# A new order of the right-hand columns, other first and last blocks, and one projection group of a slot added to x from PSUM by VectorE: window attention with a convolution on one core

## The chip, the cores and the metric

One core of a Trainium2 chip runs the kernel. The metric is the device time of one execution in microseconds, the median of three runs. Engines are named as in the profile: PE is TensorE (PEld its weight loads), DVE VectorE, ACT ScalarE, POOL GpSimd, SP the sync engine, which here only issues DMAs.

## The reference

The input x is an image of 511 x 511 positions with 192 channels in bf16. The result is

```
pe  = depthwise 3x3 convolution of x (zero border), weights dw_pe
x0  = x + pe
h   = layernorm(x0) over the channels, no scale or bias
windows of 7x7 positions: 73 x 73 windows of 49 tokens
qkv = h @ w_qkv          # 4 heads of 48
out = softmax(q k^T / sqrt(48)) v @ w_o, per window and head
return x0 + out
```

## The kernel before, in words

**Blocks.** The 73 x 73 windows are handled in blocks of up to 128 windows, one window in each partition. `_blocks` (L42) lists the lines of windows of which a block consists: (first row, first column, row step, column step, number of windows, first partition). There are 42 blocks. Blocks 0 to 35 hold two half rows of 64 windows each (columns 0 to 63). Block 36 holds row 72's half and a part of column 64, blocks 37 to 40 two pieces of columns of 64 windows each (rows 1 to 64), and block 41 the nine corners that are left: nine lines of 9 windows, 81 in all.

**What a block needs.** `load_xp` (L203) fills XP: for each window the 9 x 9 patch of x that the convolution reads, 81 partitions. It issues nine loads for each line, one for each patch column, in runs of 384 bytes, and clears patches at the image's border by a DMA of zeros (L200). There is one XP buffer. `load_x` (L248) loads x itself into X[b % 3], 14 strips in a block of two lines, and one piece for each line in a block of more than two. `store` (L300) writes the result from X in four chunks of rows, one DMA for each line and chunk. All of these wait in order in SP's queue, and each DMA uses one of eight semaphores and waits for the earlier DMA of its semaphore.

**The convolution** (`conv_mm`, L311) is a matmul for each channel, 192 in a block. Ten channels fill a `psc` buffer in PSUM, of which there are two; VectorE adds it to X (L324). Then come layernorm statistics on VectorE (L329), the inverse deviation on GpSimd (L338, L339), the norm (L344, mostly GpSimd), transposes into HO on TensorE (L354) and copies out of PSUM (L364).

**The slots.** The main loop (from L563) runs over 667 slots of eight windows. In a slot TensorE does q (L378), k (L378), v (L394), scores (L416), the product with v of the slot before (L437), the transposes of its result (L461), and up to three projection groups of the block before (`proj`, L466: four positions of all windows, L473). All these share three `ps` buffers in turn. ScalarE takes q, k and v out of PSUM (L386, L402) and does the exponential (L424); VectorE normalises (L446, L447) and copies back into HO (L462). A projection group is copied out by ScalarE (L484) and added to X by GpSimd (L488); with `direct` VectorE adds it from PSUM in two instructions (L478). `direct` is true only after the last block, for every second group.

**What runs beside the slots.** During block b the convolution, norm and transposes of block b + 1 are woven in between the slots' matmuls (`fill`), and XP and X of block b + 2 are loaded: `hook` is called four times in a slot and issues what a share of the block allows, XP once the convolution of b + 1 is done with the buffer, X by a gate on the stores if there are exactly 14 strips, and else after all stores of block b - 1. The 13 projection groups of block b - 1 fall in slots 1 to 5 of a block with 14 slots or more (`even`, L584), and between 10% and 48% of a shorter one.

**The start.** Before the loop, block 0 is convolved and normalised alone (`prepare`, L516): all statistics, then row by row the norm, the first two rows' on GpSimd and five rows' on VectorE. HO, k, pt and v are cleared ahead of that (L275 to L279).

Of the kernel before, what the change touches and what calls it, by code (L numbers as in the profile page):

```python
# [32 lines left out]
WS, NH, C, DH, S = 7, 4, 192, 48, 49  # L33
BLK, CH, KP, KT = 128, 8, 81, 96
# [4 lines left out]
_HALF = 64  # L39


def _blocks(nwr, nwc):  # L42

    full, tall = min(_HALF, nwc), min(_HALF, nwr)
    top = min(1, nwr - tall)
    halves = [(a, 0, 0, 1, full) for a in range(nwr)]
    halves += [(top, b, 1, 0, tall) for b in range(full, nwc)]
    blocks = [[h + (64 * i,) for i, h in enumerate(halves[k : k + 2])] for k in range(0, len(halves), 2)]
    if nwc > full:
        cur, p = (blocks.pop(), 64) if len(halves) % 2 else ([], 0)  # L50
        for a in [*range(top), *range(top + tall, nwr)]:
            n = nwc - full
            if p + n > BLK:
                blocks.append(cur)
                cur, p = [], 0
            cur.append((a, full, 0, 1, n, p))
            p += n
        if cur:
            blocks.append(cur)
    return blocks  # L60


class _Kernel:
# [140 lines left out]
    def load_xp(self, b):  # L204

        nc, x, XP, XPr, W, NWR, NWC = self.nc, self.x, self.XP, self.XPr, self.W, self.NWR, self.NWC
        blocks, clear, dram = _blocks(NWR, NWC), self.clear, self.dram
        for a0, b0, da, db, n, p0 in blocks[b]:
            left = [0] if b0 == 0 else []
            right = [] if b0 + (n - 1) * db < NWC - 1 else list(range(n)) if da else [n - 1]  # L210
            if left and (b == 0 or any(ln[1] for bb in blocks[:b] for ln in bb)):
                yield clear(XPr[0], p0, n if da else 1)
            if right:
                yield clear(XPr[8], p0 + right[0], len(right))
            last = a0 + (n - 1) * da
            cuts = [0] + ([1] if da and a0 == 0 else []) + ([n - 1] if da and last == NWR - 1 else []) + [n]
            for i, j in zip(cuts, cuts[1:]):
                if j <= i:
                    continue
                top, bot = a0 + i * da == 0, a0 + (j - 1) * da == NWR - 1  # L220
                if top:
                    yield clear(XP[0:9], p0 + i, j - i)
                if bot:
                    yield clear(XP[KP - 9 : KP], p0 + i, j - i)
                pr0, pr1 = (1 if top else 0), (8 if bot else 9)
                for pc in range(9):
                    q, sh = (WS - 1, -1) if pc == 0 else (0, 1) if pc == 8 else (pc - 1, 0)
                    n0, n1 = i, j
                    if pc == 0 and left:
                        n0 = j if da else i + 1  # L230
                    if pc == 8 and right:
                        n1 = i if da else j - 1
                    if n1 <= n0:
                        continue
                    dims = [[W * C, pr1 - pr0], [WS * C * (W * da + db), n1 - n0], [1, C]]
                    dst = XPr[pc, pr0:pr1, p0 + n0 : p0 + n1, :]
                    src = dram(x, WS * (a0 + n0 * da) - 1 + pr0, WS * (b0 + n0 * db + sh) + q, dims)
                    q = nc.scalar if (len(blocks[b]) > 2 and pc % 3 == 2) or (b == 0 and pc % 2) else nc.sync
                    yield lambda q=q, dst=dst, src=src: q.dma_start(out=dst, in_=src)  # L239

    def strips(self, b, r0, r1):

        W = self.W
        for a0, b0, da, db, n, p0 in _blocks(self.NWR, self.NWC)[b]:
            yield slice(p0, p0 + n), (WS * a0 + r0, WS * b0, [[WS * C * (W * da + db), n], [W * C, r1 - r0], [1, WS * C]])

    def load_x(self, b):

        nc = self.nc
        short = len(_blocks(self.NWR, self.NWC)[b]) > 2  # L250
        for r0, r1 in [(0, WS)] if short else [(r, r + 1) for r in range(WS)]:
            for p, at in self.strips(b, r0, r1):
                dst = self.X[b % 3][p, r0 * WS : r1 * WS, :].rearrange("p (r q) c -> p r (q c)", q=WS)
                q = nc.sync
                yield lambda q=q, dst=dst, src=self.dram(self.x, *at): q.dma_start(out=dst, in_=src)


    def fast(self, ctx):
        nc, tc = self.nc, self.tc
# [12 lines left out]
        o_ = pool.tile([128, 2, 2, C], BF, name="o")  # L272
        pO = _Rot([pool.tile([128, 4, C], BF, name=f"pO{i}") for i in range(2)])
        r_ = pool.tile([128, 16], F32, name="rs")
        nc.vector.memset(HO[0][:], 0.0)  # L275
        nc.gpsimd.memset(HO[1][:], 0.0)
        nc.vector.memset(k_[:], 0.0)
        for t in [pt] + vv:
            nc.vector.memset(t[:], 1.0)  # L279

        x, out, W = self.x, self.out, self.W
        NWR, NWC = self.NWR, self.NWC
# [44 lines left out]
        def ln_stat(b, i):  # L327
            s = min(2 * i, S - 2)
            nc.vector.bn_stats(  # L329
                out=bnst[:, s : s + 2, :].rearrange("p a f -> p (a f)"),  # L330
                in_=self.X[b % 3][:, s : s + 2, :].rearrange("p s c -> p c s"),
            )

        def ln_rstd(r):

            t = slice(r * WS, (r + 1) * WS)
            e = nc.gpsimd
            e.tensor_scalar(out=rstd[:, t], in0=bnst[:, t, 2], scalar1=1.0 / C, scalar2=self.eps, op0=ALU.mult, op1=ALU.add)  # L338
            e.tensor_tensor(out=rstd[:, t], in0=rstd[:, t], in1=expo[:].to_broadcast([128, WS]), op=ALU.pow)  # L339
# [159 lines left out]
        class Next:  # L499
# [15 lines left out]

            def prepare(n_):  # L516

                while n_.si < STATS:
                    ln_stat(n_.b, n_.si)
                    n_.si += 1  # L520
                for r in range(WS):
                    ln_rstd(r)
                    n_.ready.append((now[0], ln_norm(n_.b, r, nc.gpsimd if r < 2 else nc.vector)))
                    if r >= 2:
                        ln_tr(n_.b, n_.tr, n_.ready[n_.tr][1])
                        n_.tr += 1

# [24 lines left out]
            t()  # L552
        n.prepare()
        n.finish()
        sq = []
        nn = None

# [3 lines left out]
        for g in range(NG + LE + 1):  # L561
# [18 lines left out]
            def part(lo, hi, total, at=None):  # L580
                return min(total, max(0, int(((f if at is None else at) - lo) / (hi - lo) * total + 0.5)))

            pj = []
            even = b < NB and nslot >= 14  # L584
            if 1 <= b and ck >= (LE - 1 if even else LE):
                goal = 13 if b == NB else min(13, 3 * ck - 2) if even else part(0.10, 0.48, 13)
                while pdone < goal:
# [20 lines left out]
            def hook(share):  # L608

                nonlocal xpn, xln  # L610
                at = f0 + (f - f0) * share
                if n and n.conv.c == C:
                    n.stats(int(s_start + (s_goal - s_start) * share))
                while sq and sq[0][0] <= g + share:
                    _, bb, k = sq.pop(0)
                    store(bb, k)
                    stored[bb] = k + 1
                    freed[k] = g + share
                if even and 1 <= b and len(xl) == 2 * WS:
                    while xln < len(xl) and freed.get(xln // 4, NG) + 0.9 <= g + share:  # L620
                        xl[xln]()
                        xln += 1
                if n is None or n.conv.c == C:
                    goal = part(0.38 + d, 0.96 if many else 0.58 + 0.5 * d, len(xp), at)
                    while xpn < goal:
                        xp[xpn]()
                        xpn += 1
                    if b < 1 or stored.get(b - 1, 0) == len(CHUNKS):
                        goal = part(0.5, 0.7, len(xl), at)
                        while xln < goal:  # L630
                            xl[xln]()
                            xln += 1
# [2 lines left out]
                stage_A(b, ck, 0, fill if not ahead else lambda w: None, cuts)  # L635
            if 0 <= g - LE < NG:
                stage_E(*groups[g - LE], nc.vector.tensor_copy)
            def project(groups_):
                nonlocal sdone
                for s0 in groups_:  # L640
                    proj(b - 1, s0, b == NB and s0 % 8 == 0)
                    while sdone < len(CHUNKS) and CHUNKS[sdone][1] * WS <= min(S, s0 + 4):
                        sq.append((g + 0.9, b - 1, sdone))
                        sdone += 1

            first, second = max(0, len(pj) - 2), max(0, len(pj) - 1)
            if g < NG:
                hook(0.3)
                project(pj[:first])
                stage_A(b, ck, 1, fill, cuts)  # L650
                hook(0.5)
                project(pj[first:second])
            else:
                second = 0
# [276 lines left out]
```

## Time and profile before

| | |
|---|---|
| median of three runs | 3611.0 us (3599.74 to 3615.5) |
| profiled execution, its own time | 3608.29 us |
| its span | 3606.6 us |
| PE, PEld busy | 3330.4, 2941.1 us |
| DVE, ACT, POOL busy | 2504.5, 2804.7, 2063.1 us |

Busy times are sums over one profiled execution. PE's matmuls overlap each other and their ends are modelled, so a busy PE is not one at its peak. An engine's idle time before an instruction is put down to the one that released it last.

### The profile page before, as it was taken

The page shows a single profiled execution, that of the slowest core. Times are in us where ns is not written, and L with a number is a line of the kernel's source. Part 1 is how long each engine was busy: PE and PEld are TensorE (multiplying, and loading weights), DVE is VectorE, ACT ScalarE, POOL GpSimd, SP SyncE. Part 2 cuts the span into 40 slices and gives each one's busy share as a digit, 9 for nine tenths or more (in the row PEclk, how much of TensorE's full clock was granted, in tenths as well). Part 3 has the DMA queues.
Part 4 walks back from the last instruction along what each step waited for, and adds up shares of the span by engine and source line. Part 5 has one row for each costly group of instructions (what it writes and reads, how often), then busy time and mean ns, then how long its engine had stood idle before and what let it go on. Part 6 is the DMA issues. An engine that isn't in the chain of part 4 may idle for free.

```text
span 3606.6 us, 170088 instructions
## 1 busy us (share of the span) xinstructions
PE 3330.4 (92%) x77393; PEld 2941.1 (82%) x77393; DVE 2504.5 (69%) x4236; ACT 2804.7 (78%) x3512; POOL 2063.1 (57%) x1425
## 2 busy tenths in 40 slices
PE   4999999999999999999999999999999999999687
PEld 3888888888888888888888888888888888888575
DVE  6767667777776667777777766777777766666563
ACT  1788888888888888888888888888888877777575
POOL 4356655666555566566655566656665555555453
PEclk9999999999999999999999999999999998999898
DMA  6344444444434444444444444444444444444311
GB/s 145 74 101 108 115 117 116 117 113 113 103 101 101 106 112 116 119 118 114 115 104 101 101 107 112 116 117 118 114 117 103 101 101 101 101 101 105 67 32 46
DMA packets 529123, 377.39 MB, mean 105 GB/s; under 512 B 453595, under 2 KB 453787, under 8 KB 528393
## 3 DMA queue, kind: packets, MB, share of 16 engines
q1 hardware_dynamic: 521440, 363.75, 40.8%
q8 instruction: 607, 9.95, 1.2%
q10 hardware_dynamic: 6953, 2.69, 0.4%
q14 instruction: 123, 1.01, 0.1%
HBM read 265.31 MB, written 100.27 MB: 101 GB/s over the span
## 4 chain that ended last, share of the span: by engine, by line
PE 63%; DVE 15%; ACT 9%; issue 4%; POOL 3%; SPq 3%; DMA 3%; ACTq 0%; POOLq 0%; DVEq 0%
PE ps L378 19%; PE ps L473 11%; PE psc L318 9%; PE ps L394 9%; PE ps L461 7%; DVE bnst L329 6%; DVE o L447 4%; PE psc L354 4%; ACT pO L484 4%; ACT v L402 3%; SPq L239 3%; PE ps L437 2%; POOL h L344 2%; DVE HO L462 2%; PE ps L416 2%
## 5 line engine op out<-in xcount | busy, mean ns | idle before, releaser
L488 POOL TENSOR_TENSOR X<-X,pO 128x768 bf16<-128x768 bf16 (+1 forms) x539 | 845.8, 1573 | 1097.9 <-ACT pO L484 1095.5
L378 PE MATMUL ps<-HO,Wqk 96*128 96x196 bf16 (+1 forms) x7680 | 1318.4, 283 | 89.3 <-ACT pO L484 49.0
L318 PEld LDWEIGHTS <-XP 81*128 81x128 bf16 x8064 | 1014.4, 175 | 105.3 <-issue 95.5
L318 PE MATMUL psc<-T,XP 81*128 81x49 bf16 x8064 | 1036.0, 205 | 48.6 <-DMA XP<-in_x_dram 34.6
L378 PEld LDWEIGHTS <-Wqk 96*128 96x128 bf16 x7680 | 753.7, 104 | 150.6 <-issue 22.5
L324 DVE TENSOR_TENSOR X<-psc,X 128x490 bf16<-128x490 f32 x840 | 539.1, 645 | 448.9 <-PE psc L318 445.9
L386 ACT CAST k<-ps 128x784 bf16<-128x784 f32 x667 | 542.0, 813 | 243.3 <-PE ps L378 220.2
L344 POOL TENSOR_TENSOR h<-X,rstd 128x1344 bf16<-128x1344 bf16 x287 | 697.9, 2432 | 22.5
L386 ACT CAST q<-ps 128x784 bf16<-128x784 f32 x667 | 542.2, 813 | 187.2 <-PE ps L378 146.5
L394 PE MATMUL ps<-Wv,HO 96*128 96x192 bf16 x5336 | 646.6, 245 | 22.8 <-ACT q L386 19.7
L447 DVE TENSOR_TENSOR o<-ps,rs 128x768 bf16<-128x768 f32 x667 | 638.8, 958 | 23.3
L394 PEld LDWEIGHTS <-HO 96*128 96x128 bf16 x5336 | 515.0, 104 | 106.6 <-issue 69.7
L424 ACT ACTIVATE pt<-ps 128x784 bf16<-128x784 f32 x667 | 550.1, 825 | 55.8 <-PE ps L416 40.5
L402 ACT CAST v<-ps 128x768 bf16<-128x768 f32 x667 | 536.3, 804 | 69.3 <-PE ps L394 58.6
L329 DVE BATCH_NORM_STATS2 bnst<-X 128x6 f32<-128x384 bf16 x1050 | 533.9, 547 | 4.2
L462 DVE COPY HO<-ps 96x784 bf16<-96x784 bf16 x667 | 380.0, 570 | 209.5 <-PE ps L461 207.4
L484 ACT CAST pO<-ps 128x768 bf16<-128x768 f32 x498 | 397.7, 799 | 145.8 <-PE ps L473 127.5
L473 PE MATMUL ps<-Wo,HO 96*128 96x192 bf16 x4116 | 491.3, 262 | 1.4 <-DVE HO L462 0.7
L461 PEld LDWEIGHTS <-o 128*96 128x96 bf16 x5336 | 364.8, 125 | 109.3 <-DVE o L447 78.5
L339 POOL TENSOR_TENSOR rstd<-rstd,expo 128x7 f32<-128x7 f32 x294 | 439.2, 1494 | 24.5
L461 PE MATMUL ps<-ident,o 128*96 128x128 bf16 x5336 | 421.4, 222 | 24.8 <-DVE o L447 22.6
L473 PEld LDWEIGHTS <-HO 96*128 96x128 bf16 x4116 | 436.8, 186 | 1.9 <-DVE HO L462 0.9
(55 smaller groups left out, 2604.9 us busy)
## 6 DMA issues: line engine op xcount, KB each, us to landing
XP<-in_x_dram SPq DMA_DIRECT2D x644, 216.0 KB
X<-in_x_dram SPq DMA_DIRECT2D x574, 168.0 KB
out_dram<-X SPq DMA_DIRECT2D x246, 336.0 KB
XP<-in_x_dram SPq DMA_DIRECT2D x71, 212.6 KB
out_dram<-X SPq DMA_DIRECT2D x82, 168.0 KB
XP<-in_x_dram SPq DMA_DIRECT2D x12, 192.0 KB
X<-in_x_dram SPq DMA_DIRECT2D x9, 165.4 KB
XP<-in_x_dram SPq DMA_DIRECT2D x42, 30.4 KB
```

The costliest lines, as they stand in the source:

```text
L318: mm(cv.ps[:, (c % 10) * S : (c % 10 + 1) * S], lhsT=XP[0:KP, :, c], rhs=T[0:KP, c, :], start=True, stop=True)
L329: nc.vector.bn_stats(out=bnst[:, s : s + 2, :].rearrange("p a f -> p (a f)"), in_=self.X[b % 3][:, s : s + 2, :].rearrange("p s c -> p c s"),)
L344: eng.tensor_tensor(out=h[:, :, :], in0=self.X[b % 3][:, t, :], in1=rstd[:, t].unsqueeze(2).to_broadcast([128, WS, C]), op=ALU.mult)
L378: mm(ps[:, ab * 512 + i * m * S : ab * 512 + (i + 1) * m * S], lhsT=self.Wqk[kt][0:KT, which * 2 + ab, :], rhs=HO[b % 2][0:KT, kt, ck * CH ...
L386: nc.scalar.copy(out=dst[:, :, 0:TOK], in_=two_bank(ps, TOK))
L394: mm(ps[:, col : col + C], lhsT=HO[b % 2][0:KT, kt, w : w + 2, :].rearrange("p w s -> p (w s)"), rhs=self.Wv[kt][0:KT, :], start=(kt == 0) ...
L402: eng(out=v_[:].rearrange("p (b j) h e -> p b (j h) e", b=2)[:, :, :, 0:DH], in_=two_bank(ps, 2 * C).rearrange("p b (g d) -> p b g d", d=DH),)
L424: nc.scalar.activation(out=pt[:, 0 : 16 * S].rearrange("p (b n) -> p b n", b=2), in_=two_bank(ps, 8 * S), func=ACTF.Exp, scale=SCALE)
L447: nc.vector.tensor_tensor(out=o_[:].rearrange("p b q (h d) -> p b (q h) d", d=DH), in0=ov[:, :, :, 0:DH], in1=r_[:].rearrange("p (b g) -> ...
L461: mm(ev, lhsT=o_[:, sl, Q, kt * KT : (kt + 1) * KT], rhs=ident[:], start=True, stop=True, is_transpose=True)
L473: mm(ps[:, col : col + C], lhsT=HO[b % 2][0:KT, kt, :, s0 + i], rhs=self.Wo[kt][0:KT, :], start=(kt == 0), stop=(kt == 1))
L488: nc.gpsimd.tensor_tensor(out=xv, in0=xv, in1=o[:, 0:n, :], op=ALU.add)
```

## The change

- `_blocks`: columns 64 to 72 are taken whole from row 1 to row 71 and packed end to end into blocks of 128, a column running over into the next block. Blocks 36 and 40 hold two lines, 37 to 39 three, all of them column pieces of 14 to 71 windows; block 40 has 127 windows. Block 41 holds row 72's half (64 windows) and the two corners of rows 0 and 72 (nine each), 82 windows.
- `strips`: a line is cut into a part of a multiple of 16 windows and the rest, for loads of X and for stores.
- `load_x`: column blocks load all seven rows of a piece at once, as short blocks did. XP loads go to ScalarE's queue in block 0 only.
- The XP loads of block b + 2 are spread up to 62% of the block instead of 96% where it has more than two lines.
- `even` also holds for a last block of 11 slots.
- Of three projection groups in a slot, the first goes directly from PSUM to X by VectorE; in the last block every second group does too.
- `prepare`: statistics row by row, norms of rows 0, 2, 4 and 6 on VectorE and of 1, 3 and 5 on GpSimd. All clearing of HO, k, pt and v is on GpSimd, HO[1] only after block 0 is prepared.

```diff
 def _blocks(nwr, nwc):
-    full, tall = min(_HALF, nwc), min(_HALF, nwr)
-    top = min(1, nwr - tall)
+    full = min(_HALF, nwc)
+    n = nwc - full
     halves = [(a, 0, 0, 1, full) for a in range(nwr)]
-    halves += [(top, b, 1, 0, tall) for b in range(full, nwc)]
     blocks = [[h + (64 * i,) for i, h in enumerate(halves[k : k + 2])] for k in range(0, len(halves), 2)]
-    if nwc > full:
-        cur, p = (blocks.pop(), 64) if len(halves) % 2 else ([], 0)
-        for a in [*range(top), *range(top + tall, nwr)]:
-            n = nwc - full
-            if p + n > BLK:
-                blocks.append(cur)
-                cur, p = [], 0
-            cur.append((a, full, 0, 1, n, p))
-            p += n
+    if n:
+        last, p = (blocks.pop(), _HALF) if nwr % 2 else ([], 0)
+        cur, q = [], 0
+        for b in range(full, nwc):
+            a = 1
+            while a < nwr - 1:
+                m = min(nwr - 1 - a, BLK - q)
+                cur.append((a, b, 1, 0, m, q))
+                a, q = a + m, q + m
+                if q == BLK:
+                    blocks.append(cur)
+                    cur, q = [], 0
         if cur:
             blocks.append(cur)
+        blocks.append(last + [(a, full, 0, 1, n, p + i * n) for i, a in enumerate((0, nwr - 1))])
...
-                    q = nc.scalar if (len(blocks[b]) > 2 and pc % 3 == 2) or (b == 0 and pc % 2) else nc.sync
+                    q = nc.scalar if b == 0 and pc % 2 else nc.sync
...
     def strips(self, b, r0, r1):
...
-            yield slice(p0, p0 + n), (WS * a0 + r0, WS * b0, [[WS * C * (W * da + db), n], [W * C, r1 - r0], [1, WS * C]])
+            for i, m in ((0, n - n % 16), (n - n % 16, n % 16)):
+                if m:
+                    at = (WS * (a0 + i * da) + r0, WS * (b0 + i * db), [[WS * C * (W * da + db), m], [W * C, r1 - r0], [1, WS * C]])
+                    yield slice(p0 + i, p0 + i + m), at
...
     def load_x(self, b):
-        short = len(_blocks(self.NWR, self.NWC)[b]) > 2
+        lines = _blocks(self.NWR, self.NWC)[b]
+        short = len(lines) > 2 or any(ln[2] for ln in lines)
...
-        nc.vector.memset(HO[0][:], 0.0)
-        nc.gpsimd.memset(HO[1][:], 0.0)
-        nc.vector.memset(k_[:], 0.0)
+        nc.gpsimd.memset(HO[0][:], 0.0)
+        nc.gpsimd.memset(k_[:], 0.0)
         for t in [pt] + vv:
-            nc.vector.memset(t[:], 1.0)
+            nc.gpsimd.memset(t[:], 1.0)
...
-                while n_.si < STATS:
-                    ln_stat(n_.b, n_.si)
-                    n_.si += 1
-                for r in range(WS):
-                    ln_rstd(r)
-                    n_.ready.append((now[0], ln_norm(n_.b, r, nc.gpsimd if r < 2 else nc.vector)))
-                    if r >= 2:
+                for r in range(WS + 1):
+                    if r < WS:
+                        while n_.si < min(STATS, ((r + 1) * WS + 1) // 2):
+                            ln_stat(n_.b, n_.si)
+                            n_.si += 1
+                        ln_rstd(r)
+                    if r:
+                        n_.ready.append((now[0], ln_norm(n_.b, r - 1, nc.vector if r % 2 else nc.gpsimd)))
+                    if r > 1:
                         ln_tr(n_.b, n_.tr, n_.ready[n_.tr][1])
                         n_.tr += 1
...
         n.prepare()
         n.finish()
+        nc.gpsimd.memset(HO[1][:], 0.0)
...
-            even = b < NB and nslot >= 14
+            even = b < NB and nslot >= 8
...
-                    goal = part(0.38 + d, 0.96 if many else 0.58 + 0.5 * d, len(xp), at)
+                    goal = part(0.38 + d, 0.62 if many else 0.58 + 0.5 * d, len(xp), at)
...
-            def project(groups_):
+            def project(groups_, direct=False):
                 nonlocal sdone
                 for s0 in groups_:
-                    proj(b - 1, s0, b == NB and s0 % 8 == 0)
+                    proj(b - 1, s0, direct or b >= NB - 1 and s0 % 8 == 0)
...
-                project(pj[:first])
+                project(pj[:first], True)
```

## Rows read from the trace of the kernel before

**Rows 1.** The page's first part: busy time, share of the span, instructions of each engine.

```profile
PE 3330.4 (92%) x77393; PEld 2941.1 (82%) x77393; DVE 2504.5 (69%) x4236; ACT 2804.7 (78%) x3512; POOL 2063.1 (57%) x1425
```

**Rows 2.** Stretches, cut at each block's first L424: length, busy times, clock, DMA share, GB/s.

```profile
1736.80:1818.90 82.10, 78.40 (x1856) 69.24 (x1854) 58.81 (x101) 66.92 (x85) 49.00 (x34) 1.00 0.44 110
...
3144.80:3232.60 87.80, 80.70 (x1859) 71.57 (x1857) 59.26 (x102) 67.06 (x84) 49.00 (x34) 0.95 0.43 103
...
3319.40:3441.60 122.20, 82.11 (x1866) 72.24 (x1863) 59.28 (x102) 67.66 (x85) 49.06 (x34) 0.85 0.27 55
3525.00:3575.70 50.70, 45.41 (x975) 35.67 (x974) 17.96 (x31) 40.15 (x54) 19.88 (x13) 0.97 0.20 50
3575.70:3606.60 30.90, 13.63 (x146) 13.13 (x146) 8.71 (x18) 4.83 (x7) 9.85 (x6) 0.67 0.21 53
```

**Rows 3.** Waits from 3390 to 3442 us: total, times, longest.

```profile
PE psc L318 <- DMA XP<-in_x_dram: 33.0, 1, 33.0
```

**Rows 4.** SP's queue in blocks 37 and 39 and the tail: start, duration, issues.

```profile
3180.40 4.23 SPq L255 DMA_DIRECT2D X<-in_x_dram  x6
3184.98 35.41 SPq L239 DMA_DIRECT2D XP<-in_x_dram  x18
...
3427.94 4.33 SPq L239 DMA_DIRECT2D XP<-in_x_dram  x6
...
3587.75 16.39 SPq L303 DMA_DIRECT2D out_dram<-X  x36
```

**Rows 5.** The chain of waits at the end of block 37: start, duration.

```profile
3218.95 5.58 DMA XP<-in_x_dram
```

**Rows 6.** A stretch behind that landing, columns as in rows 2.

```profile
3224.00:3233.00 9.00, 8.28 (x135) 8.21 (x136) 3.45 (x6) 3.25 (x4) 0.00 (x0) 0.52 0.01 2
```

**Rows 7.** Groups over the span: busy, mean ns of one, idle before it and its releasers.

```profile
L378 PE MATMUL ps<-HO,Wqk 96*128 96x196 bf16 (+1 forms) x7680 | 1318.4, 283 | 89.3 <-ACT pO L484 49.0 <-ACT v L402 21.6 <-DVE HO L364 7.6
...
L478 DVE TENSOR_TENSOR X<-ps,X 128x384 bf16<-128x384 f32 (+1 forms) x13 | 6.4, 537 | 6.1 <-PE ps L473 6.1
```

**Rows 8.** TensorE in a projection slot of block 20: start, duration.

```profile
1756.08 0.25 PE L378 MATMUL ps<-HO,Wqk 96*128 96x196 bf16 x1 [0.31 <-ACT pO L484]
...
1757.62 0.91 PE L473 MATMUL ps<-Wo,HO 96*128 96x192 bf16 x8
...
1760.22 0.25 PE L394 MATMUL ps<-Wv,HO 96*128 96x192 bf16 x1
```

**Rows 9.** VectorE in the same slot.

```profile
1758.68 0.67 DVE L324 TENSOR_TENSOR X<-psc,X 128x490 bf16<-128x490 f32 x1 [0.29 <-PE psc L318]
```

**Rows 10.** VectorE at the start.

```profile
36.12 6.88 DVE L275 MEMSET HO<- 128x8192 uint32 x1 [1.68 <-issue]
...
45.84 1.18 DVE L324 TENSOR_TENSOR X<-psc,X 128x490 bf16<-128x490 f32 x2
...
62.71 11.74 DVE L329 BATCH_NORM_STATS2 bnst<-X 128x6 f32<-128x384 bf16 x25
75.06 1.56 DVE L344 TENSOR_TENSOR X<-X,rstd 128x1344 bf16<-128x1344 bf16 x1 [0.61 <-POOL rstd L339]
...
86.77 1.56 DVE L344 TENSOR_TENSOR X<-X,rstd 128x1344 bf16<-128x1344 bf16 x1 [1.37 <-POOL rstd L339]
```

**Rows 11.** A stretch at the start, columns as in rows 2.

```profile
40.00:40.50 0.50, 0.00 (x0) 0.00 (x0) 0.50 (x1) 0.00 (x0) 0.50 (x1) 1.00 0.52 161
```

**Rows 12.** GpSimd at the start.

```profile
34.44 13.75 POOL L276 MEMSET HO<- 128x16384 bf16 x1 [25.52 <-DMA X<-in_x_dram]
...
65.03 1.50 POOL L339 TENSOR_TENSOR rstd<-rstd,expo 128x7 f32<-128x7 f32 x1
66.61 2.43 POOL L344 TENSOR_TENSOR X<-X,rstd 128x1344 bf16<-128x1344 bf16 x1
...
75.30 2.66 POOL L339 TENSOR_TENSOR rstd<-rstd,expo 128x7 f32<-128x7 f32 x1
```

**Rows 13.** GpSimd in the tail.

```profile
3588.05 6.52 POOL L488 TENSOR_TENSOR X<-X,pO 128x768 bf16<-128x768 bf16 x4 [0.33 <-ACT pO L484]
```

More of the change, by code (lines that the diff above doesn't have):

```diff
@@ L42, in _blocks @@
 def _blocks(nwr, nwc):
-    full, tall = min(_HALF, nwc), min(_HALF, nwr)
-    top = min(1, nwr - tall)
+    full = min(_HALF, nwc)
+    n = nwc - full
+    assert 2 * n <= _HALF
     halves = [(a, 0, 0, 1, full) for a in range(nwr)]
-    halves += [(top, b, 1, 0, tall) for b in range(full, nwc)]
     blocks = [[h + (64 * i,) for i, h in enumerate(halves[k : k + 2])] for k in range(0, len(halves), 2)]
-    if nwc > full:
-        cur, p = (blocks.pop(), 64) if len(halves) % 2 else ([], 0)
-        for a in [*range(top), *range(top + tall, nwr)]:
-            n = nwc - full
-            if p + n > BLK:
-                blocks.append(cur)
-                cur, p = [], 0
-            cur.append((a, full, 0, 1, n, p))
-            p += n
+    if n:
[10 more added lines that the diff above has]
+                    cur, q = [], 0
         if cur:
             blocks.append(cur)
+        blocks.append(last + [(a, full, 0, 1, n, p + i * n) for i, a in enumerate((0, nwr - 1))])
     return blocks
```

## The prediction

> **What bounds the kernel now.** I read the page first: TensorE is busy 92% of the span, ScalarE 78%, VectorE 69% [rows 1]. That says that only holes in TensorE's work are worth much, so I cut the trace at the end of each block's first exponential (L424) and read the blocks beside each other [rows 2]. An ordinary block of sixteen slots takes 82.1 us with TensorE busy for 78.4 of it: there is little to win there. A block near the end takes 87.8 us, block 39 takes 122.2 us for the same 82.1 us of TensorE work, and the last 30.9 us hold 13.6 us of it. So the losses lie at the ends: block 39, the tail, and (seen in the engine timelines) the first 100 us.
>
> In block 39 the waits name the culprit: the convolution's matmuls of block 41 wait 33.0 us for their patches XP [rows 3]. SP's queue shows why. A normal column block's 18 XP loads take 35.41 us; for block 41 (nine short lines, 81 loads and clears of borders) the queue is still issuing at 3427.9 to 3432.3, six loads in 4.33 us [rows 4], when TensorE has waited some 30 us already.
>
> **The change part by part.**
>
> *Block 41's order.* It falls from nine lines to three (row 72 and two corners of nine), so from 81 XP loads to 27 with six clears. XP loading can start once the convolution has read the old patches: in block 37 at 3184.98, which is 40.2 us after that block's start (3144.8) [rows 2, 4]. Costed at the column rate for the nine long loads (35.41/18 = 1.97 us) and at 4.33/6 = 0.72 us for the 24 short ones, it takes 17.7 + 17.3 = 35.0 us, done 75 us into block 39. Wanted it is at about 78.5: in block 37 the last XP landed at 3218.95 + 5.58 = 3224.5 [rows 5] and the matmul had waited for it 1.2 us, so 3223.3. Hence the 33 us stall goes, and block 39 becomes an 87.8 us block: 122.2 − 87.8 = **−34.4 us**. The estimate is only 3 us ahead of the need, and the rest of X's load may stand in front, so the bounds are −36 and, if a third of the stall stays, −23.
>
> *Blocks 36 to 40.* Columns of 71 windows are packed end to end, so a block has two or three lines. The XP bytes stay the same, in 18 to 27 loads instead of 18. But X's load changes its place. Before, X came in 14 strips, let through as stores freed the buffer: the last six stood directly ahead of XP and were through at 3184.6 [rows 4]. Now such a block's X comes in four to six large pieces which no longer pass that gate; by the code they go out from half of the block on, in between the XP loads. What is late next is XP. A strip costs 4.23/6 = 0.70 us, all fourteen 9.9 us; about 55% of a block's X is queued ahead of its last XP load, 5.5 us, and what stood ahead of XP before (up to 2 us of draining) goes away. So XP lands some 4 us later than now, and in block 37 it was already 1.2 us late. At five boundaries (XP of blocks 36 to 40): **+20 us**. Below: 0, where the slack of a block swallows it; above: all of X ahead, 9.9 us, plus 1 us for the additional loads, times five, +55. I take a value below the middle since some boundaries have slack now. TensorE stood mostly at the lower of its two clock levels (granted 0.52, 1.2 GHz) for 9 us behind that late landing [rows 6]: a repeat costs up to 4.5 us, which the upper bound covers. Stores of these blocks grow from 8 to 16 to 24 pieces on SP, but they are issued in the first 40 us of a block, where that queue waits for projections anyway: 0; without that cover, some 12 extra issues of 0.46 us (the short stores of the tail [rows 4]), 5.5 us a block.
>
> *The first projection group of slots 2 to 5, to VectorE.* In 4 slots of each of 41 blocks, 164 times, a ScalarE copy and a GpSimd add become two VectorE adds from PSUM of 0.537 us [rows 7]. What would be gained? TensorE's only wait in such a slot is 0.31 us at its start, for ScalarE's copy of the slot's *last* group [rows 8], in all 49.0 us [rows 7]; that copy starts when its own matmuls end and isn't touched. What would be lost? In the slot shown, TensorE finishes the group at 1757.62 + 0.91 = 1758.53, and VectorE is idle then. The adds would end at about 1759.65; TensorE wants the buffer for V at 1760.22 [rows 8]: hidden by 0.57 us. Behind them on VectorE waits a convolution add, at 1758.68 [rows 9], now 1 us later; the two psc buffers give it one group of ten channels, some 2 us. So **0**. If both covers are gone, a slot pays what overshoots; I bound it by the 0.3 us of the one stall the slot has, 49 us in all; a gain is excluded down to some −10 us (0.06 us a slot from an emptier ScalarE).
>
> *The start.* VectorE clears HO for 6.88 us and then k, pt and v before it takes the first convolution add at 45.84 [rows 10]. GpSimd takes these now. X of block 0 had landed by about 40.0: the DMA share drops to 0.52 there before the next block's load fills the queue [rows 11]. So the adds start at about 40.2: **−5.6 us**, at most −9.7 (all from 36.12 on), at least 0 if something else holds the first add. GpSimd needs 13.75 us for one HO [rows 12] and it was doing just that in this place, so the new one is hidden; the second HO moves behind the first block's preparation, where GpSimd has no work for that block's slots until the next norms: 0, and if needed 13.75 us at most.
>
> *Norms of block 0.* Now the statistics go row by row, and four norms on VectorE alternate with three on GpSimd (before, five and two). Before, the last norm ends at 86.77 + 1.56 = 88.33, 25.6 us after the first statistic at 62.71 [rows 10]. By GpSimd's steps taken alone, 2.0 us to the first of them, seven of 1.8 (a scaling and a power of 1.50) and three norms of 2.43 [rows 12] make 21.9 us: −3.7. The rows speak against it: the power took 2.66 us when a VectorE norm of 1.56 us ran beside it [rows 10, 12]. Four such meetings of 1.16 us make 26.5: +0.9, and about as much comes back since VectorE's copies no longer queue behind a last norm. I take 0, between −3.7 and +1.5. The Trainium skill (SBUF — State Buffer, section "SBUF: two separate sides") says that a VectorE instruction with two SBUF inputs and a GpSimd one hold their shared port pair exclusively, and the loser waits in full. By that rule the sum has 0 here, by durations taken alone −3.7; the trace agrees with the rule (2.66 against 1.50 us).
>
> *Last block and tail.* Block 41's projections of block 40 are spread three to a slot instead of six at once; TensorE idles 5.3 of its 50.7 us [rows 2], I take half: **−2.5 us** (0 to −5). The tail ends with 36 small stores, 16.39 us on SP up to 3604.1 [rows 4]. Now there are 12. The last data come from GpSimd at 3588.05 + 6.52 = 3594.57 [rows 13], and three stores of 0.46 us follow: 3596.0, so −8; I take **−7.5 us** (−5 to −9).
>
> Sum: −34.4 + 20 + 0 − 5.6 + 0 − 2.5 − 7.5 = −30.0. The profiled execution took 3608.3 us (span 3606.6), so 3578; the median of the runs is 2.7 us above it: about **3580 us**.
>
> **The rivals.** (1) XP stays in time in the column blocks: no +20, so 3560. For it: some boundaries have slack; against: block 37 has none. (2) The other side: XP so late that each of the five boundaries pays more than 10 us (50 us of gains divided by five; that is the point from which it decides). At 10.9 us late plus 3 us of low clock each, 70 − 50 = +20: 3631. For it: SP issues in order, and the clock row; against: only part of X stands ahead. (3) VectorE's direct adds delay TensorE in each of the 164 slots by 0.3 us: +49 − 30, 3630. Against: the margins of 0.57 and 1 us. (4) The change doesn't do what it says for block 41: its 33 loads and clears are still late, with a third to a half of the stall left, 3592 to 3597.
>
> **How the numbers follow.** Chances: forecast 0.52, (1) 0.15, (2) 0.10, (3) 0.07, (4) 0.16. The time is the forecast's. About 0.5%, 18 us, is what this measurement can tell from none (the three runs lie 16 us apart). Faster by more than that, below 3593: most of the forecast (0.47), (1), a quarter of (4), 0.66. Slower, above 3629: 0.07 of (2) and 0.04 of (3), 0.11. The rest, 0.23. The range: down to 3552, which is (1) with its better bounds, and up to 3608, which takes in (4) and leaves out (2) and (3) with the worst of the forecast. The forecast's own range is 3562 to 3597.
>
> **What would show it.** Right: block 39 near 88 us and no XP wait of tens of us; the first L324 near 40 us; the span ending about 4 us after the last GpSimd add; slots 2 to 5 still near 7.1 us; waits of several us for XP at the boundaries of blocks 35 to 39. Wrong: XP waits above 10 us there, block 39 above 95 us, or ordinary blocks off 82 us by more than 0.3 (40 blocks make 12 us of it).

## The result, and the profile after

The changed kernel takes 3636.6 us, the median of four runs (3633.1 to 3646.9). The kernel before, run beside it, takes 3607.1 (3599.7 to 3615.5). The ratio is 1.0082, its 95% interval 1.0066 to 1.0098: slower by 0.8%. Forecast were 3580 us and a range of 3552 to 3608. The kernel got slower where it was to get faster, and its time lies above the range.

The profiled spans are 3634.8 us after and 3606.6 before, 28.2 us apart. Both traces were cut at the end of each block's first exponential, which gives this balance:

| stretch | before, us | after, us | difference | term of the prediction |
|---|---|---|---|---|
| up to the first exponential | 101.1 | 98.7 | −2.4 | −5.6 (start), 0 (norms) |
| blocks 0 to 33 | 2783.1 | 2786.4 | +3.3 | 0 (direct adds) |
| blocks 34 to 38 | 435.2 | 496.5 | **+61.3** | **+20** |
| block 39 | 122.2 | 96.9 | −25.3 | −34.4 |
| block 40 | 83.4 | 83.3 | −0.1 | 0 |
| block 41 | 50.7 | 48.1 | −2.6 | −2.5 |
| tail | 30.9 | 24.9 | −6.0 | −7.5 |

Every term that was not put at zero has the sign forecast. One size is off by 41 us, and that is enough to turn the result round. First the page's busy times after, against [rows 1]:

```profile
PE 3342.1 (92%) x77393; PEld 2949.7 (81%) x77393; DVE 2657.0 (73%) x4567; ACT 2671.1 (73%) x3343; POOL 1802.4 (50%) x1262
```

VectorE gained 152 us of work, ScalarE lost 134 and GpSimd 261. TensorE has the same 77393 matmuls. None of that says why the kernel is slower. The stretches do, with columns as in [rows 2]: an ordinary block, blocks 34, 37, 39 and 41, the tail, and then the two stretches around a boundary in block 37:

```profile
1736.80:1818.80 82.00, 78.51 (x1855) 69.34 (x1854) 62.52 (x110) 63.73 (x80) 42.37 (x30) 1.00 0.45 111
...
2885.10:2981.50 96.40, 82.87 (x1832) 71.56 (x1831) 61.70 (x108) 64.17 (x80) 42.50 (x30) 0.93 0.47 94
3183.90:3284.80 100.90, 80.52 (x1867) 71.43 (x1866) 62.65 (x109) 63.88 (x80) 42.40 (x30) 0.91 0.44 90
3381.60:3478.50 96.90, 82.47 (x1868) 73.30 (x1866) 62.75 (x109) 63.86 (x80) 42.40 (x30) 0.92 0.31 70
3561.80:3609.90 48.10, 43.54 (x975) 34.43 (x974) 26.34 (x48) 34.37 (x45) 6.56 (x4) 1.00 0.20 52
3609.90:3634.80 24.90, 13.39 (x146) 12.83 (x146) 8.68 (x18) 4.81 (x7) 9.79 (x6) 0.76 0.28 66
...
3263.00:3278.00 15.00, 0.29 (x2) 0.16 (x3) 0.28 (x1) 0.22 (x1) 0.00 (x0) 0.55 0.78 141
3278.00:3282.00 4.00, 4.00 (x42) 4.00 (x43) 1.15 (x2) 0.81 (x1) 0.00 (x0) 0.55 0.05 8
```

The ordinary block is unchanged (82.0 against 82.1). Block 37 is 13.1 us longer for the same TensorE work, and the row before the last shows how: TensorE does nothing for some 14 us while the DMA engines are 0.78 busy. Behind that it works at a granted clock of 0.55, near its lower level of 1.2 GHz, for 4 us; in the kernel before there was a like stretch of 9 us [rows 6], so that the difference is the stand. The waits of TensorE after, in six stretches (2925 to 2940, 3076 to 3088, 3170 to 3186, 3270 to 3287, 3370 to 3384 and 3465 to 3480), name what it stood for:

```profile
PE ps L423 <- issue: 4.5, 1, 4.5
...
PE psc L325 <- DMA XP<-in_x_dram: 11.4, 1, 11.4
...
PE psc L325 <- DMA X<-in_x_dram: 6.3, 1, 6.3
...
PE psc L325 <- DMA X<-in_x_dram: 14.4, 1, 14.4
...
PE psc L325 <- DMA XP<-in_x_dram: 7.1, 1, 7.1
...
PE psc L325 <- DMA XP<-in_x_dram: 8.4, 1, 8.4
```

Blocks 35 to 39 each end in such a wait: 11.4 us, 6.3, 14.4, 9.9 (in two) and 8.4. In three of the five it is for XP (in block 38 7.1 us for XP, then 2.8 for VectorE's add of X), and in the other two the last thing to come is X itself. In the kernel before, the waits for XP in blocks 35 to 38 come to 1.6 us:

```profile
PE psc L318 <- DMA XP<-in_x_dram: 1.6, 2, 1.2
```

Block 34 after has no wait of several us for X or XP. It has two waits of 8.5 us together in which the profile shows nothing that TensorE waits for ("issue").

SP's queue after, in block 37 and in the tail (start, duration, issues), stands against [rows 4]:

```profile
3225.12 22.24 SPq L243 DMA_DIRECT2D XP<-in_x_dram  x14
3247.41 1.29 SPq L263 DMA_DIRECT2D X<-in_x_dram  x1
3248.74 9.66 SPq L243 DMA_DIRECT2D XP<-in_x_dram  x4
3258.45 1.93 SPq L263 DMA_DIRECT2D X<-in_x_dram  x1
3260.42 5.62 SPq L243 DMA_DIRECT2D XP<-in_x_dram  x7
3266.61 0.64 SPq L263 DMA_DIRECT2D X<-in_x_dram  x1
3267.30 1.61 SPq L243 DMA_DIRECT2D XP<-in_x_dram  x2
3268.96 1.66 SPq L263 DMA_DIRECT2D X<-in_x_dram  x2
...
3622.25 9.59 SPq L310 DMA_DIRECT2D out_dram<-X  x12
```

Before, X was through 40 us into the block and XP had the queue for itself. After, XP starts at the same place (41.2 us in), X's five pieces stand in between, and the last of XP and X is issued 85.0 to 86.7 us in. Wanted it is at about 78.5, by the prediction's own number. The tail's stores are the 12 forecast, in 9.59 us instead of the 16.39 of 36.

### The profile page after: what moved, and what is told of

Read it like the earlier page. It is cut to its first block, busy times and chain, and to the rows that moved or that the text cites. A ratio compares the mean times of both kernels' runs of the same rounds, so it can differ in the third digit from the quotient of the medians.

```text
span 3634.8 us, 170511 instructions
## 1 busy us (share of the span) xinstructions
PE 3342.1 (92%) x77393; PEld 2949.7 (81%) x77393; DVE 2657.0 (73%) x4567; ACT 2671.1 (73%) x3343; POOL 1802.4 (50%) x1262
## 4 chain that ended last, share of the span: by engine, by line
PE 58%; DVE 14%; ACT 8%; SPq 8%; issue 4%; DMA 4%; POOL 3%; ACTq 0%; POOLq 0%; DVEq 0%
PE ps L385 18%; PE ps L480 10%; PE psc L325 9%; PE ps L401 8%; PE ps L468 6%; SPq L243 6%; DVE bnst L336 5%; ACT pO L491 4%; DVE o L454 4%; PE psc L361 3%; DMA X<-in_x_dram 3%; ACT v L409 3%; POOL h L351 2%; PE ps L444 2%; DVE HO L469 2%
## 5 line engine op out<-in xcount | busy, mean ns | idle before, releaser
L385 PE MATMUL ps<-HO,Wqk 96*128 96x196 bf16 (+1 forms) x7680 | 1324.8, 284 | 90.3 <-ACT pO L491 49.6
L495 POOL TENSOR_TENSOR X<-X,pO 128x768 bf16<-128x768 bf16 x370 | 566.0, 1535 | 1408.1 <-ACT pO L491 1404.9
L385 PEld LDWEIGHTS <-Wqk 96*128 96x128 bf16 x7680 | 756.6, 104 | 152.3 <-issue 24.4
L453 DVE RECIPROCAL rs<-ps 128x16 f32<-128x16 f32 x667 | 167.4, 251 | 355.1 <-PE ps L444 317.8
## 6 DMA issues: line engine op xcount, KB each, us to landing
X<-in_x_dram SPq DMA_DIRECT2D x504, 168.0 KB
out_dram<-X SPq DMA_DIRECT2D x84, 168.0 KB
```

The costliest lines, as they stand in the source:

```text
L385: mm(ps[:, ab * 512 + i * m * S : ab * 512 + (i + 1) * m * S], lhsT=self.Wqk[kt][0:KT, which * 2 + ab, :], rhs=HO[b % 2][0:KT, kt, ck * CH ...
L495: nc.gpsimd.tensor_tensor(out=xv, in0=xv, in1=o[:, 0:n, :], op=ALU.add)
```

## The experiments

Three theories were held against each other. **A**: both XP and X are wanted at the boundary, so each byte of X that is let in behind the start of XP delays it, whichever comes first. **B**: the 27 loads of XP that packed columns need are themselves slower than 18. **C**, the prediction's counting: only the part of X that stands ahead of the last XP load costs time.

**X early, packed order kept.** X of the column blocks goes out in four groups of window rows, and again through the gate that lets them go as stores free the buffer, ahead of XP:

```
-        for r0, r1 in [(0, WS)] if short else ...
+        for r0, r1 in [(0, 2), (2, 4), (4, 6), (6, WS)] if short else ...
...
-                if even and 1 <= b and len(xl) == 2 * WS:
-                    while xln < len(xl) and freed.get(xln // 4, NG) + 0.9 <= g + share:
+                if even and 1 <= b:
+                    per = 4 if nn and plain(b + 2) else max(1, len(xl) // 4)
+                    while xln < len(xl) and freed.get(xln // per, NG) + 0.9 <= g + share:
```

> The changed kernel, with x of the column blocks and of the last block loaded again in the early place: in four chunks of rows, each let through when the store of the same chunk has gone, ahead of XP. Theory A (the whole load of x now shares the stretch with XP, and both are needed at the boundary, so some 12 us come on top of XP's 38): blocks 34 to 38 go from 96 to 105 us back to 85 to 90, some 50 us less in all, 3575 to 3590. Theory B (27 smaller XP loads of the packed columns are slower in themselves): the boundaries still pay 10 us or more each, above 3620.

Measured: 3575.4 us (3570.3 to 3584.9) beside 3609.7 for the kernel before, ratio 0.9909 (0.9883 to 0.9935). The stretches of blocks 37 and 39 in this kernel:

```profile
3150.70:3240.60 89.90, 81.06 (x1867) 71.99 (x1866) 62.70 (x109) 63.91 (x81) 42.36 (x30) 0.95 0.43 101
...
3326.50:3412.30 85.80, 79.11 (x1866) 70.04 (x1863) 62.89 (x110) 63.91 (x81) 42.38 (x30) 1.00 0.33 79
```

And its SP queue in block 37:

```profile
3165.30 9.93 SPq L310 DMA_DIRECT2D out_dram<-X  x8
3175.27 6.10 SPq L263 DMA_DIRECT2D X<-in_x_dram  x10
3181.86 5.22 SPq L310 DMA_DIRECT2D out_dram<-X  x8
3187.12 5.42 SPq L263 DMA_DIRECT2D X<-in_x_dram  x10
3193.05 37.88 SPq L243 DMA_DIRECT2D XP<-in_x_dram  x27
```

X is through before XP starts, and XP starts as far into the block as before (42.4 us). Blocks 34 to 39 are shorter than in the changed kernel by 8.3, 13.4, 10.1, 11.0, 10.9 and 11.1 us, 64.8 together. The last five, 56.5 us, are those that ended in a wait for XP or X; block 34 had only its "issue" waits, 8.5 us, of which 4.9 are left. This is A for most of the loss. B is not refuted, but it is small: all 27 loads take 37.88 us where 18 took 35.41 [rows 4], 2.5 us more, and waits for XP of 4.9 us in block 35 and 2.6 in block 37 are left.

**The kernel before, with X of its column blocks in whole pieces.** The order and everything else stay as they were:

```
-        short = len(_blocks(self.NWR, self.NWC)[b]) > 2
+        lines = _blocks(self.NWR, self.NWC)[b]
+        short = len(lines) > 2 or any(ln[2] for ln in lines)
```

> The kernel before in its old order, with only x of its column blocks loaded as whole pieces, which takes that load out of the early place. Theory A: the boundaries of blocks 35 to 39 are late by 8 to 14 us each, some 45 us more than before, 3645 to 3660. Theory B: the XP loads are those of before, so nothing moves, 3600 to 3615.

Measured: 3652.8 us (3649.3 to 3655.9), ratio 1.0111 (1.0088 to 1.0135). Its stretch of block 37:

```profile
3174.00:3273.90 99.90, 82.79 (x1862) 73.34 (x1861) 59.36 (x102) 67.28 (x85) 49.02 (x34) 0.91 0.44 91
```

And its SP queue in block 37:

```profile
3215.50 26.70 SPq L239 DMA_DIRECT2D XP<-in_x_dram  x13
3242.30 2.14 SPq L256 DMA_DIRECT2D X<-in_x_dram  x1
3244.49 14.65 SPq L239 DMA_DIRECT2D XP<-in_x_dram  x5
...
```

Two pieces of X suffice: blocks 34 to 38 take 89.3, 100.3, 97.5, 99.9 and 94.8 us, 481.8 against 435.2, while block 39 stays at 122.3. The old order with its 18 loads shows most of the loss, 46.6 us, without any packing: A a second time. The edit makes X both late and coarse. No run loads it late in small strips, so that the share of the size of the pieces stays open. The queue also shows where a piece of X is paid for: the XP loads behind it take 14.65/5 = 2.93 us of the queue each, those ahead of it 26.70/13 = 2.05.

**X behind the last XP load.** In the changed kernel, X waits until all of XP has been issued:

```
-                    if b < 1 or stored.get(b - 1, 0) == len(CHUNKS):
+                    if (b < 1 or stored.get(b - 1, 0) == len(CHUNKS)) and xpn == len(xp):
```

> The changed kernel with all pieces of x of block b + 2 issued after its last XP load. Theory C, the prediction's counting (only pieces of x ahead of the last XP load cost): XP lands some 6 us earlier and the boundaries pay 3 to 6 us less each. Theory A (x itself is what is late too): the boundaries keep within 3 us of 15 to 22, and the wait is named after x instead of XP.

Measured: 3643.2 us (one run). Blocks 34 to 39 take 96.0, 106.6, 102.9, 102.1, 98.4 and 98.4 us: no block gains more than a fraction of a microsecond over the changed kernel, most lose. SP's queue in block 37 of this kernel:

```profile
3226.82 37.83 SPq L243 DMA_DIRECT2D XP<-in_x_dram  x27
3265.01 3.92 SPq L263 DMA_DIRECT2D X<-in_x_dram  x5
```

VectorE's first convolution add behind it:

```profile
3283.07 1.24 DVE L331 TENSOR_TENSOR X<-psc,X 128x490 bf16<-128x490 f32 x2 [12.74 <-DMA X<-in_x_dram]
```

And the DMA engines in between, by stretches:

```profile
3270.00:3275.00 5.00, 1.51 (x20) 1.44 (x19) 0.33 (x1) 0.81 (x1) 0.00 (x0) 0.84 1.05 185
3275.00:3280.00 5.00, 0.00 (x0) 0.00 (x0) 0.00 (x0) 0.00 (x0) 0.00 (x0) 0.50 0.81 137
3280.00:3285.00 5.00, 1.20 (x15) 1.15 (x15) 1.24 (x2) 0.00 (x0) 0.00 (x0) 0.50 0.11 22
```

XP now stands ahead of all of X and is not waited for in this block. The wait has moved to the other operand: the add that takes the convolution into X stands 12.7 us, and in blocks 35, 36, 38 and 39 it stands 14.8, 13.6, 11.4 and 8.7. By C each boundary would be 3 to 6 us shorter, and none is shorter by more than 0.4, so C falls, as far as one run tells. A's "within 3 us" holds for the slots that hold the boundary in three of the five blocks (35 to 39: 27.2, 21.2, 21.5, 19.2 and 18.0 us, in the changed kernel 22.1, 15.6, 22.6, 19.5 and 17.3); two are 5 us longer. The rows also show what a block's X costs. SP issues it in 3.92 us, but the DMA engines stay busy for some eleven microseconds behind that (share 1.05, then 0.81, then 0.11). X is 14 strips of 168.0 KB, 2.4 MB; at the 185 GB/s of the full stretch that is an estimated 13 us.

**No direct adds.** The changed kernel with the first projection groups by ScalarE and GpSimd again:

```
-                project(pj[:first], True)
+                project(pj[:first])
```

> The changed kernel with the first projection group of a slot copied by ScalarE and added by GpSimd again. The prediction's 0 for the direct adds: ordinary blocks stay within 0.2 us of 82.0 and the time within 5 us of the changed kernel. The rival (VectorE's adds delay TensorE by 0.3 us a slot): 49 us less.

Measured: 3638.5 us (3632.0 to 3647.3), ratio to before 1.0069 (1.0044 to 1.0093), where the changed kernel has 1.0082. An ordinary block takes 82.1 us. The group of TensorE's first projection matmul (L385, its idle time at the end) reads:

```profile
L385 PE MATMUL ps<-HO,Wqk 96*128 96x196 bf16 (+1 forms) x7680 | 1326.1, 285 | 89.3 <-ACT pO L491 49.0 <-ACT v L409 21.4 <-DVE HO L371 6.4
```

The same group in the changed kernel, and the direct adds themselves:

```profile
L385 PE MATMUL ps<-HO,Wqk 96*128 96x196 bf16 (+1 forms) x7680 | 1324.8, 284 | 90.3 <-ACT pO L491 49.6 <-ACT v L409 21.5 <-DVE HO L371 7.7
...
L485 DVE TENSOR_TENSOR X<-ps,X 128x384 bf16<-128x384 f32 (+1 forms) x350 | 178.4, 551 | 53.3 <-PE ps L480 50.9 <-ACT pO L491 1.2 <-PE psc L325 1.1
```

The idle time for ScalarE's last copy is 49.0 us without the direct adds and 49.6 with them. Of the 350 adds of 0.551 us this kernel keeps 26, in the last block and behind it. Moving the other 324 to VectorE is worth nothing that these runs can tell, and the +3.3 us of blocks 0 to 33 are not theirs: without them these blocks take 2793.1 us in this profile.

**X early and all norms of block 0 on VectorE.** The first experiment, with the split of the norms taken out:

```
-    ... ln_norm(n_.b, r - 1, nc.vector if r % 2 else nc.gpsimd)
+    ... ln_norm(n_.b, r - 1, nc.vector)
```

> e1_early_x with all seven norms of block 0 on VectorE. If the collision of a GpSimd norm with a VectorE norm (3.78 us instead of 1.56 in the changed kernel) is what eats the gain of the new order at the start: the last norm ends some 24.5 us after the first statistic instead of 28.1, and the first exponential comes 3 to 4 us earlier, near 95 us. If the order of statistics is what counts: it stays near 98.5. In all 3570 to 3573.

Measured: 3574.2 us (3567.8 to 3579.2), ratio 0.9905 (0.9885 to 0.9925). Beside the first experiment's 0.9909 that is no difference in the total. The start of the profile shows one. VectorE at the start of the changed kernel, where the norms alternate:

```profile
42.98 1.24 DVE L331 TENSOR_TENSOR X<-psc,X 128x490 bf16<-128x490 f32 x2 [8.03 <-DMA X<-in_x_dram]
...
59.90 3.32 DVE L336 BATCH_NORM_STATS2 bnst<-X 128x6 f32<-128x384 bf16 x7
63.75 1.56 DVE L351 TENSOR_TENSOR X<-X,rstd 128x1344 bf16<-128x1344 bf16 x1 [0.53 <-POOL rstd L346]
...
69.05 3.78 DVE L351 TENSOR_TENSOR X<-X,rstd 128x1344 bf16<-128x1344 bf16 x1 [0.51 <-POOL rstd L346]
...
84.23 3.78 DVE L351 TENSOR_TENSOR X<-X,rstd 128x1344 bf16<-128x1344 bf16 x1 [0.89 <-POOL rstd L346]
```

GpSimd in the same place:

```profile
68.99 2.43 POOL L351 TENSOR_TENSOR X<-X,rstd 128x1344 bf16<-128x1344 bf16 x1
71.39 1.51 POOL L345 TENSOR_SCALAR rstd<-bnst 128x7 f32<-128x7 f32 x1
```

VectorE's last norm in the experiment's kernel, with all norms on VectorE:

```profile
82.77 1.56 DVE L351 TENSOR_TENSOR X<-X,rstd 128x1344 bf16<-128x1344 bf16 x1 [0.66 <-POOL rstd L346]
```

And its first exponential, on ScalarE:

```profile
94.27 0.83 ACT L431 ACTIVATE pt<-ps 128x784 bf16<-128x784 f32 x1
```

In the changed kernel three of VectorE's four norms take 3.78 us, each beside one of GpSimd's of 2.43, and the last ends 28.1 us after the first statistic. In the experiment the last ends 25.1 us after the first (which starts at 59.20), and the first exponential starts at 94.27 instead of 97.91 (97.55 in the first experiment).

**X early, the start of the kernel before.** The first experiment with the old clears and the old order of statistics and norms:

```
-        nc.gpsimd.memset(HO[0][:], 0.0)
-        nc.gpsimd.memset(k_[:], 0.0)
+        nc.vector.memset(HO[0][:], 0.0)
+        nc.gpsimd.memset(HO[1][:], 0.0)
+        nc.vector.memset(k_[:], 0.0)
-            nc.gpsimd.memset(t[:], 1.0)
+            nc.vector.memset(t[:], 1.0)
...
-                for r in range(WS + 1):
-                    if r < WS:
-                        while n_.si < min(STATS, ((r + 1) * WS + 1) // 2):
...
-                        ln_rstd(r)
-                    if r:
-                        ... ln_norm(n_.b, r - 1, nc.vector if r % 2 else nc.gpsimd)
+                while n_.si < STATS:
...
+                for r in range(WS):
+                    ln_rstd(r)
+                    ... ln_norm(n_.b, r, nc.gpsimd if r < 2 else nc.vector)
...
-        nc.gpsimd.memset(HO[1][:], 0.0)
```

> e1_early_x with the clearing and the preparation of block 0 as before the change. The start alone: first exponential at 101 us instead of 98.4, the rest the same; the prediction had put 5.6 us on it.

Measured: 3586.7 us (one run, the highest run of the first experiment is 3584.9). VectorE's first convolution add starts at 46.54, and the first exponential stands here on ScalarE:

```profile
100.94 0.83 ACT L432 ACTIVATE pt<-ps 128x784 bf16<-128x784 f32 x1
```

In the first experiment the exponential starts at 97.55. So the new start is worth 3.4 us there by the trace. The 11 us in the total are one run against four and show no more than that: by the profiles, blocks 34 to 38, which the start does not touch, take 454.0 us here and 442.8 there. Two profiles of the same blocks can lie that far apart.

**X early, the old order of blocks.** The first experiment with the block order of the kernel before (in `_blocks`, the diff of the change reversed):

```
-    full = min(_HALF, nwc)
-    n = nwc - full
+    full, tall = min(_HALF, nwc), min(_HALF, nwr)
+    top = min(1, nwr - tall)
...
+    halves += [(top, b, 1, 0, tall) for b in range(full, nwc)]
```

> e1_early_x with the lists of windows of the kernel before. The order alone: block 39 takes 120 us again (33 us waiting for XP of block 41) instead of 85.8, the tail some 5 us longer, so 35 to 42 us above e1_early_x, 3610 to 3618. If packing the columns costs something that the early x hides only in part, blocks 34 to 38 are shorter here than in e1_early_x by more than 2 us each.

Measured: 3614.3 us (3606.4 to 3618.6), ratio 1.0011 (0.9995 to 1.0026). Its block 39:

```profile
3310.90:3439.60 128.70, 81.51 (x1859) 72.18 (x1857) 63.00 (x110) 63.78 (x81) 42.40 (x30) 0.82 0.21 52
```

And TensorE's wait in it:

```profile
PE psc L321 <- DMA XP<-in_x_dram: 41.5, 1, 41.5
```

Beside the first experiment, the new order is worth 3614.3 − 3575.4 = 38.9 us. It saves 128.7 − 85.8 = 42.9 in block 39 and costs 442.8 − 428.5 = 14.3 over blocks 34 to 38 (83.7, 88.2, 84.8, 85.8 and 86.0 us here). Of the remaining 10 us, the tail has 6.5 and block 40 has 2.2. Four of the five blocks from 34 to 38 are 2.8 to 4.4 us shorter here, which the expectation named as the sign that packing costs something. Block 39's wait is 41.5 us here, not the 33.0 of [rows 3]. That block 41's XP loads no longer share ScalarE's queue is a likely reason; no run separates it.

With this run the place of X and the packing can be told apart. Blocks 34 to 38 take, in us (X early: this kernel and the first experiment's; X late, in whole pieces: the second experiment's and the changed kernel):

| | X early | X late | difference |
|---|---|---|---|
| old order | 428.5 | 481.8 | 53.3 |
| packed order | 442.8 | 496.5 | 53.7 |
| difference | 14.3 | 14.7 | |

So B has its part: the packed order costs some 14 us wherever X is. With X early, the packed XP holds SP's queue for 38.60, 33.73 and 37.88 us in blocks 35 to 37, the old order's for 30.57, 34.05 and 34.06, and the old order has no wait for XP in them. Each sum is of one profile, and the sixth experiment shows that two such sums can lie 11 us apart. The 53 are well clear of that, the 14 are not; but block 34 is longer in the packed order in every profile (88.1 to 88.3 us against 83.7 with X early, 95.9 to 96.4 against 89.3 with X late).

## Why the prediction was wrong

**Blocks 36 to 40, the step that failed.** It says that "about 55% of a block's X is queued ahead of its last XP load, 5.5 us", and "So XP lands some 4 us later than now". It counts as a cost only what stands ahead of XP, and it counts by the time that SP needs to issue strips (14 at 0.70 us, 9.9). The first is what failed, and it put +20 where +61.3 was measured: at the boundary the convolution's add needs X as well as XP, so all of X counts. The second is too low besides, since X fills the DMA engines for an estimated 13 us and not 9.9. With X ahead of XP, in the gate's stretch, the five boundaries that had waited for data (four of those costed, and that of block 41) are 56.5 us cheaper, 11.3 each. With X behind XP they are no cheaper. Two of the prediction's own signs of being wrong came true: waits above 10 us (11.4 and 14.4), and block 39 above 95 us (96.9).

Of the 61.3 us, some 40 are waits for XP or X in blocks 35 to 38 (42.0 against 1.6), 10.1 a boundary. 7.0 are the "issue" waits in block 34 (8.5 against 1.5). Most of the remainder is TensorE at the lower clock: its busy time over the five blocks is 414.0 us instead of 404.2 for the same work, almost all of the difference in blocks 34 to 36, where the mean granted clock is 0.93, 0.86 and 0.90 (before 0.98, 0.95 and 0.93). The bound of +55 had all of X, 10.9 us at each of five boundaries, and no term for these two; the prediction says that it covers the clock. Seen the other way, 46.6 of the 61.3 us come with the late X alone (the second experiment) and 14.7 with the packed order on top of it.

**Rival (2) came nearest.** 61.3/5 = 12.3 us more a boundary on the mean, four of the five at 10 or over, where it decides from 10. But block 34 is one of the four and pays in "issue" waits, and in blocks 36 and 37 it is X that comes last, not XP. Its time of 3631 is 6 us from the measured one, in part by luck: it had 70 us of cost against 50 of gains, measured are 61.3 against 33.1. It got a chance of 0.10 since "only part of X stands ahead", which is the sentence that failed.

**Block 41's order: −25.3 in place of −34.4.** The mechanism was right: the wait of 33.0 us is 8.4 now. What is left is the same loss once more, at a sixth boundary: X of block 41 goes in between its XP, which the prediction named in its bound of −23 and left out of its sum. XP holds the queue from 3423.01 to 3467.67, 44.7 us, where 35.0 were costed, and the term that is furthest off is the clears of borders: six at 0.72 us are 4.3, and they take 16.8. The last two of them, in the changed kernel behind a piece of X and in the first experiment's with X out of the way:

```profile
3452.68 7.90 SPq L204 DMA_DIRECT2D XP<-T  x2
...
3395.87 2.66 SPq L204 DMA_DIRECT2D XP<-T  x2
```

With X early, block 39 takes 85.8 us, 36.4 less than before, at the bound of −36.

**The start: −2.4 in place of −5.6, with the norms.** The clears left VectorE as described, and the first add moved from 45.84 [rows 10] to 42.98, not to 40.2. VectorE's wait there is for X, and its queue takes four semaphore events for it from 41.0 to 42.9. The norms cost 0.5 us net where 0 was forecast, but not by the forecast's steps: from the first statistic to the last norm it takes 28.1 us instead of 25.6, where 26.5 were expected, and about 2 come back behind that. Three times a VectorE norm met one of GpSimd's and took 3.78 us instead of 1.56, while the prediction let GpSimd alone lose. Without these meetings the start gains another 3.3 us (94.27 against 97.55).

**Right:** the direct adds at 0 (the fourth experiment; ordinary blocks at 82.0 us), the last block at −2.6 for −2.5, and the tail at −6.0 for −7.5: three stores follow the last GpSimd add as forecast, but they begin 1.0 us after it and take 2.12 us, not three times 0.46.

With X early the change is worth what it was forecast to be worth: 3575 us, and 3574 with the norms on VectorE as well, which the runs cannot tell apart.

## What to carry to other kernels

When an edit changes the shape of a transfer, look for the conditions elsewhere that ask for the old shape: here a gate tested for the old number of pieces, and X silently fell to a later branch. When a transfer moves into the stretch of another, count all of it, by what it occupies on the DMA engines (here an estimated 13 us) rather than by its issue time (3.92 us), against the moment at which both are wanted; putting the one ahead of the other only renames the wait. And look for a place where the queue has room before giving up the edit: four lines turned a loss of 0.8% into a gain of 0.9%.

## What the runs showed of the hardware that was not expected

- **A collision that delays VectorE.** In the kernel before, it was GpSimd's power that lost beside a VectorE norm (2.66 against 1.50 us). Here GpSimd's norm starts at 68.99, VectorE's at 69.05, and VectorE's ends at 72.83, 1.4 us after GpSimd's is through at 71.42. In turn GpSimd's next scaling takes 1.51 us, where it takes 0.21 elsewhere in the same start. The Trainium skill (SBUF — State Buffer, section "SBUF: two separate sides") says that whichever of the two starts first keeps the shared port pair for its whole instruction. The rows agree with it, in both directions.
- **Loads that slow one another.** Behind one large piece of X an XP load of the same size held SP's queue for 2.93 us instead of 2.05, and a pair of clears for 7.90 us instead of 2.66.
- **Waits that stay open.** In block 34 TensorE stands 4.5 us, near 2929, and 4.0 more near 2958, with "issue" as the only cause that the profile gives. With X early one of 4.9 us remains, at 2928; the kernel before has 1.5 us there. The profile's view of the DMA lists instruction loads as a queue of their own, q8, which brought 32 of 16 KB from 2700 to 2880, one every 5.6 us. Nothing came on it from 2920 to 2931.3; one load came between 2931.3 and 2934, and TensorE went on at 2933.87. Nothing came from 2948.4 to 2959.7, while the main queue took 0.81 of the DMA engines; one load came between 2959.7 and 2962.5, and TensorE went on at 2962.48. This order of events fits instruction loads that came late, but that q8 feeds TensorE is not shown, and why the loads were late is open. All six profiles of the packed order have a wait of 4.5 to 4.9 us in block 34, and the three of the old order have 1.3 to 1.5 us there.
